# Two attention-and-MLP layers on one core: another table of planner settings, found by a wider search

## The chip, the cores and the metric

The kernel runs on one core of a Trainium2 chip. The metric is device time in microseconds (us) for one execution, and the median of several executions is compared. The measured runs of the kernel before took 1413.7, 1416.55 and 1415.16 us, median 1415.16 us.

## The reference

Input is one sequence of 2048 tokens of 512 features in bf16. Two layers with the same weights follow each other; each is an attention block and an MLP block, both on a layernormed input and both added to the residual:

```
x = x + A(layernorm(x))      # A: 32 heads of 16 features, softmax over 2048 keys, then wo
x = x + B(layernorm(x))      # B: gelu(h @ w1 + b1) @ w2 + b2, 1792 hidden features
x = x + A(layernorm(x))
x = x + B(layernorm(x))
```

Every head needs 2048 x 2048 scores and as many exponentials, twice over. With heads of only 16 features the exponentials weigh as much as the matmuls.

## The kernel before

**The work.** The kernel plans itself when it is built: coroutines put forward operations, a planner (`_Sched.run`, line 517) keeps a clock for each engine, picks the next operation for the engine that can start first, and writes it at the end of that engine's list. On the chip each engine runs its own list in that order, held only by semaphores. So the whole kernel is a static order of some 45,000 instructions, and the planner's choices are its only freedom.

**Cells.** The scores are cut into 4096 cells, in passes. A pass is a layer, a segment of queries (512 of them, the last segment in two halves of 256) and a group of heads; a cell is a pass, one tile of 128 keys and one of four strips of 32 rows of the TensorE array. A cell is one matmul of 512 columns (line 1723, `ps<-qp,kt`) into one bank of PSUM. Its exponential is made in one of two ways:
- On ScalarE (line 2401, `exps`): one ACTIVATE takes the two or three cells of a slot of banks, `128x1024` or `128x1536`, and writes tiles `pt` (or room lent by `kt`, `v` and `g`). There are two such slots, one of three banks and one of two that gets a third bank later.
- On VectorE (line 1997, `dfirst`): a TENSOR_SCALAR turns the scores into 16-bit integers whose bits read as a coarse exponential. Three more planes are made by adding constants to them, mostly on GpSimd (line 2245), a few on VectorE (line 2247). The four planes, each against its own multiple of V (tiles `vc`, line 1651), are summed to the exponential times V.

Then TensorE multiplies by V (line 2468, `pvs`): one matmul for an ACT cell, four for a cell made on VectorE, four side by side in column strips of the array. Projections, wo and the MLP (all line 728, `quads`) run beside attention in the same column strips, some pieces of them in row strips beside the scores (line 1246, `strip`). Where TensorE would be idle, the planner puts in matmuls that compute nothing and keep it busy (line 1711, `fill`); a column strip that has nothing to do in a PV round gets a matmul with zeros (line 2476).

**Words used below.** A slot of TensorE is one stream of 512 columns, by up to four matmuls side by side. A turn is a change between row strips (scores) and column strips (all else). A step is a score group and what stands after it on TensorE up to the next group.

**What sets the order.** 34 constants of the planner (`NAMES`: how many evacuations may be ahead, when a VectorE cell may join a score group, how early PV is taken, and so on) are not constant: `ROWS` holds sets of values, and `PIECES` names the set for each of the 100 equal parts of the 4096 cells. `take` (line 1760) counts scored cells and calls `turn` (line 1756) at each part's end:

```
    def turn(self):
        self.piece += 1
        globals().update(zip(NAMES, ROWS[PIECES[self.piece]]))
```

The kernel before has 45 sets and a list of 100 numbers.

Of the kernel before, what the change touches and what calls it, by code (L numbers as in the profile page):

```python
# [99 lines left out]
         "ALONE", "AHEAD", "PSHIFT", "QUEUE", "SOLO", "BACK", "SIDE", "BOTH", "DMAX", "GMAX", "PMORE", "DUMORE", "GRACE", "PPS", "WAIT", "SOFT",  # L100
         "CLOSE", "LEAST",)
ROWS = (
# [45 lines left out]
)  # L148
PIECES = (36, 37, 18, 29, 2, 43, 11, 29, 41, 15, 37, 38, 0, 37, 31, 25, 13, 23, 16, 40, 30, 37, 25, 29, 6, 13, 0, 16, 13, 14, 44, 0, 4, 15,
          0, 17, 4, 18, 5, 10, 1, 1, 42, 28, 17, 38, 37, 35, 41, 32, 42, 0, 33, 13, 41, 6, 33, 13, 12, 42, 41, 25, 3, 0, 27, 41, 43, 43,  # L150
          19, 8, 37, 6, 38, 16, 33, 6, 36, 37, 20, 35, 41, 21, 24, 37, 7, 4, 9, 15, 25, 24, 8, 21, 37, 22, 31, 34, 26, 12, 39, 31)
CLOSE = 0.35
BOTH = 1
DMAX = 2
# [563 lines left out]
class _Plan:  # L718
# [1041 lines left out]
    def take(self, c):  # L1760
        self.scored += 1
        self.left[c[0]] -= 1
        self.due[c[0]] += 1
        if self.piece + 1 < len(PIECES) and self.scored * len(PIECES) >= (self.piece + 1) * self.total:
            self.turn()
# [823 lines left out]
```

## Time and profile before

| what | us |
|---|---|
| median of the measured runs | 1415.16 (1413.7 to 1416.55) |
| the profiled execution itself | 1413.11 |
| its span, first to last instruction | 1411.3 |
| TensorE (PE) busy | 1382.2, 98% |
| ScalarE (ACT) busy | 1385.1, 98% |
| VectorE (DVE) busy | 1271.7, 90% |
| GpSimd (POOL) busy | 989.7, 70% |

The profiled execution took 2.05 us less than the median, and its span lies 1.8 us inside its own time. PE and ACT are both at 98%, but such a share hides short waits: an ACTIVATE counts as busy until its last result is written, while the next one may start before that. So the distance from one start to the next tells more than the share.

### The profile page before, as it was taken

What the parts mean: (1) busy time and instruction counts of PE and PEld (TensorE: products, weight loads), DVE (VectorE), ACT (ScalarE), POOL (GpSimd) and SP (SyncE); (2) the same over time, 40 slices, a digit from 0 to 9 for tenths busy, and PEclk for the clock granted to TensorE, in tenths of its full rate; (3) what the DMA queues carried; (4) which work ended last, traced back from release to release, by engine and by line L of the source; (5) the groups of instructions that cost most, each with busy time, mean ns of one, the idle gap of its engine ahead of it and who ended that gap; (6) DMA issues with size and microseconds to landing.
All of it is one profiled execution on the core that took longest, in us unless ns stands there. A gap on an engine that the chain in (4) does not pass through costs nothing.

```text
span 1411.3 us, 44915 instructions
## 1 busy us (share of the span) xinstructions
PE 1382.2 (98%) x19487; PEld 411.7 (29%) x19487; DVE 1271.7 (90%) x2500; ACT 1385.1 (98%) x1404; POOL 989.7 (70%) x1239
## 2 busy tenths in 40 slices
PE   8999999999999999999999999999999999999999
PEld 3222222222222222222222222222222222344345
DVE  8999999989999899998999889999988979999794
ACT  7999999999999999999999999999999999999995
POOL 0579787768887588775778868556757874877671
PEclk9999999999999999999999999999999999999999
DMA  5200001124121331114211133101133114101112
GB/s 154 62 2 2 2 2 32 39 77 128 32 62 32 106 98 40 46 39 136 69 35 50 32 114 90 47 16 31 39 103 95 31 44 131 59 20 40 29 36 77
DMA packets 122305, 80.36 MB, mean 57 GB/s; under 512 B 36732, under 2 KB 121084, under 8 KB 122108
## 3 DMA queue, kind: packets, MB, share of 16 engines
q1 hardware_dynamic: 122108, 77.49, 19.5%
q8 instruction: 153, 2.51, 0.7%
q14 instruction: 44, 0.36, 0.1%
HBM read 65.67 MB, written 4.19 MB: 50 GB/s over the span
## 4 chain that ended last, share of the span: by engine, by line
PE 48%; ACT 40%; DVE 11%; POOL 1%; DMA 1%; issue 0%
ACT pt L2401 36%; PE ps L2468 17%; PE ps L1723 16%; PE ps L728 15%; DVE dp L1997 2%; ACT v L2401 1%; DVE kt L1997 1%; DVE v L1997 1%; ACT g L1390 1%; DVE stats L865 1%; ACT g L2401 1%; DVE xln L896 1%; DMA wr<-in_B_w_dram 1%; DVE xf L1997 0%; DVE xt L1089 0%; ACT kt L2401 0%
## 5 line engine op out<-in xcount | busy, mean ns | idle before, releaser
L2401 ACT ACTIVATE pt<-ps 128x1024 bf16<-128x1024 f32 (+1 forms) x1264 | 1236.4, 1153 | 3.7 <-PE ps L1723 2.6
L2245 POOL INT64_ADD dp<-dp x600 | 486.5, 820 | 127.0 <-DVE dp L1997 35.5
L1723 PE MATMUL ps<-qp,kt 32*128 32x512 bf16 x4096 | 547.2, 384 | 10.4 <-ACT pt L2401 7.6
L1997 DVE TENSOR_SCALAR dp<-ps 128x512 uint16<-128x512 f32 x611 | 404.8, 679 | 32.4 <-PE ps L1723 29.5
L1723 PEld LDWEIGHTS ps<-qp,kt 32*128 32x128 bf16 x4096 | 138.0, 91 | 567.7 <-ACT pt L2401 484.4
L2468 PE MATMUL ps<-pt,v 128*17 128x512 bf16 (+1 forms) x3009 | 281.2, 358 | 1.2 <-ACT pt L2401 0.5
L2245 POOL INT64_ADD kt<-kt x235 | 189.9, 812 | 96.2 <-DVE kt L1997 39.0
L2468 PE MATMUL ps<-dp,vc 128*17 128x512 bf16 (+1 forms) x2025 | 222.5, 361 | 1.5 <-POOL v L2245 1.1
L2245 POOL INT64_ADD v<-v x186 | 150.9, 814 | 67.8 <-DVE v L1997 31.2
L1997 DVE TENSOR_SCALAR kt<-ps 128x512 uint16<-128x512 f32 x239 | 160.8, 682 | 20.2 <-PE ps L1723 18.3
L1997 DVE TENSOR_SCALAR v<-ps 128x512 uint16<-128x512 f32 x186 | 124.9, 681 | 14.3 <-PE ps L1723 13.4
L728 PE MATMUL ps<-xf,wr 128*32 128x512 bf16 (+1 forms) x1792 | 128.0, 364 | 0.0
L2468 PE MATMUL ps<-kt,vc 128*17 128x512 bf16 (+1 forms) x897 | 121.2, 338 | 1.2 <-POOL dp L2245 0.9
L728 PE MATMUL ps<-wr,g 128*32 128x512 bf16 x1408 | 105.3, 383 | 0.4 <-DMA wr<-in_B_w_dram 0.2
L2468 PE MATMUL ps<-dp,v 128*17 128x512 bf16 (+1 forms) x675 | 94.6, 361 | 3.8 <-DVE xt L1089 3.1
L2468 PE MATMUL ps<-v,vc 128*17 128x512 bf16 (+1 forms) x654 | 97.1, 350 | 1.0 <-POOL v L2245 0.6
L2245 POOL INT64_ADD q<-q x89 | 72.9, 819 | 32.0 <-DVE q L1997 17.5
L2468 PEld LDWEIGHTS ps<-pt,v 128*17 128x17 bf16 x3009 | 71.1, 88 | 78.0 <-issue 58.3
L2245 POOL INT64_ADD xf<-xf x65 | 53.0, 815 | 51.4 <-DVE xf L1997 36.2
L1372 DVE TENSOR_SCALAR g<-ps,hb1t 128x512 bf16<-128x512 f32 (+1 forms) x112 | 79.0, 707 | 4.9 <-PE ps L728 2.4
L2468 PEld LDWEIGHTS ps<-dp,vc 128*17 128x17 bf16 x2025 | 58.8, 89 | 52.9 <-issue 26.8
L1997 DVE TENSOR_SCALAR q<-ps 128x512 uint16<-128x512 f32 x94 | 63.5, 682 | 8.3 <-PE ps L1723 7.8
(149 smaller groups left out, 1697.7 us busy)
## 6 DMA issues: line engine op xcount, KB each, us to landing
wr<-in_B_w_dram SPq DMA_DIRECT2D x174, 256.0 KB, 3.0
wr<-in_A_wqkv_dram SPq DMA_DIRECT2D x24, 256.0 KB, 3.1
x<-in_A_x_dram SPq DMA_DIRECT2D x7, 512.0 KB, 4.2
wr<-in_A_wo_dram SPq DMA_DIRECT2D x10, 256.0 KB, 3.6
kept<-x SPq DMA_DIRECT2D x4, 512.0 KB, 3.8
x<-kept SPq DMA_DIRECT2D x4, 512.0 KB, 4.1
out_dram<-x SPq DMA_DIRECT2D x16, 128.0 KB, 1.8
q<-in_B_w_dram SPq DMA_DIRECT2D x3, 512.0 KB, 4.4
```

Source lines behind the costliest of these rows:

```text
L728: return [lambda e, a=a: e.matmul(out[32 * a:32 * a + 32, :], lhsT=lhsT[:, 32 * a:32 * a + 32], rhs=rhs, start=start, stop=stop, tile_posi ...
L865: yield _Op("dve", 0.66, lambda e, t=t, src=src: e.bn_stats(T["STATS"][:, t, :], src), reads=[key], writes=["ST.%d" % t], prio=prio)
L896: return _Op("dve", 0.41, lambda e: e.tensor_scalar(T["XLN"][:, x, :], T["X"][:, t % XT, :], T["RSTD"][:, t:t + 1], T["NMR"][:, t:t + 1], ...
L1372: yield _Op("dve", 0.21 + n / 966, lambda e, fc=fc, pb=pb: e.tensor_scalar(T["G"][:, fc, q], pb, T["HB1T"][:, fc:fc + 1], None, op0=ALU.ad ...
L1390: lambda e, g=g: e.activation(out=g, in_=g, func=ACT.Gelu_apprx_tanh), reads=gk, writes=gk, prio=2)
L1723: return (lambda e: e.matmul(o, lhsT=lhsT, rhs=rhs, start=True, stop=True, tile_position=(32 * a, 0)), ["K%d.%d.%d" % (l, gb, kt // 4), "Q ...
L1997: yield _Op("dve", 0.682, lambda e: e.tensor_scalar(u, self.bank(b), E_SCALE, E_BIAS, op0=ALU.mult, op1=ALU.add), reads=["B.%d" % b], writ ...
L2245: op = _Op("pool", PFIX + PWORD * 128 * n * (1 + both), lambda e: e.int64_add(dst, src, by * PACKED), reads=reads, writes=writes)
L2401: yield _Op("act", EXPC + 0.4267 * n, lambda e, src=src, dst=dst: e.activation(out=dst, in_=src, func=ACT.Exp, scale=0.25), reads=["B.%d" ...
L2468: op.fns.append(lambda e, o=o, lhsT=q[0][0][m], rhs=q[0][1][:, n * m:n * m + n], a=a, st=st, sp=sp: e.matmul(o, lhsT=lhsT, rhs=rhs, start= ...
```

## The change

The values in `ROWS` and the list `PIECES` are replaced by those of another search over the planner's settings, one that kept 13 lists and tried 34 candidates at each turn instead of 6 and 28. There are now 47 sets; many are the old ones in other places. No code, no operation and no cost of the planner is touched. Two lines more in the table move every later line down by 2: line 2401 of before is line 2403 of after.

```
 ROWS = (
+    (0.5, 0.1, 0.7, 0.2, 18, 10, 2, 6, 1, 1, 2, 2, 5, 0.3, 0.4, 2, 3.5, 24, 3, 4, 0.4, 1.0, 0, 1, 2, 3, 1, 2, 0.3, 2, 0.15, 0.0, 0.35, 3,),
...
-    (0.5, 0.15, 0.7, 0.2, 18, 10, 2, 6, 1, 1, 2, 2, 5, 0.3, 0.4, 2, 3.5, 24, 3, 4, 0.4, 1.0, 0, 1, 2, 3, 1, 2, 0.3, 2, 0.15, 0.0, 0.35, 99,),
...
-PIECES = (36, 37, 18, 29, 2, 43, 11, 29, 41, 15, 37, 38, 0, 37, 31, 25, 13, 23, 16, 40, 30, 37, 25, 29, 6, 13, 0, 16, 13, 14, 44, 0, 4, 15,
+PIECES = (42, 42, 44, 29, 6, 8, 46, 45, 25, 39, 12, 17, 36, 19, 15, 32, 26, 26, 9, 26, 35, 26, 20, 43, 24, 25, 16, 14, 3, 30, 34, 12, 0,
```

What it does to the engines' lists is shown at three places. The first is ACT's list in the opening, four exponentials behind the last of the three copies of `kt` (line 1005). Before:

```order
L2401 ACTIVATE pt<-ps 128x1536
L2401 ACTIVATE pt<-ps 128x1024 x3
L2401 ACTIVATE pt<-ps 128x1536
L2401 ACTIVATE pt<-ps 128x1024 x4
L2401 ACTIVATE pt<-ps 128x2x512
L2401 ACTIVATE pt<-ps 128x1024 x5
L2401 ACTIVATE pt<-ps 128x2x512
L2401 ACTIVATE pt<-ps 128x3x512
L2401 ACTIVATE pt<-ps 128x2x512
```

The same place after, from the instruction at which the two lists part:

```order
L2403 ACTIVATE pt<-ps 128x3x512
L2403 ACTIVATE pt<-ps 128x2x512
L2403 ACTIVATE pt<-ps 128x1024 x4
L2403 ACTIVATE pt<-ps 128x3x512
L2403 ACTIVATE pt<-ps 128x2x512
L2403 ACTIVATE pt<-ps 128x3x512
L2403 ACTIVATE pt<-ps 128x1024 x6
L2403 ACTIVATE pt<-ps 128x2x512
L2403 ACTIVATE pt<-ps 128x3x512
```

An exponential of three cells (`128x1536` or `128x3x512`) stands here 3 times among 18 before, and 4 times among 17 after. Over the whole list there are 1342 exponentials before (1180 of two cells, 162 of three) and 1337 after (1156 of two, 180 of three, 1 of one).

The second place is ACT's end. `g<-g` is the gelu of the part before the last, which waits until all exponentials are made. Before:

```order
L2401 ACTIVATE pt<-ps 128x1024 x9
L2401 ACTIVATE v<-ps 128x1536 x2
L2401 ACTIVATE pt<-ps 128x1536 x2
L2401 ACTIVATE pt<-ps 128x3x512
L1390 ACT_TABLE_LOAD
L1390 ACTIVATE g<-g 128x7x256 x2
```

After:

```order
L2403 ACTIVATE v<-ps 128x1536 x2
L2403 ACTIVATE pt<-ps 128x1536 x2
L2403 ACTIVATE pt<-ps 128x512
L1392 ACT_TABLE_LOAD
L1392 ACTIVATE g<-g 128x7x256 x2
```

The last exponential takes one cell instead of three; what follows it is the same.

The third place is PE's list from the last score group (`ps<-qp,kt`) on. `17x256` is PV for a segment of 256 queries, so eight of them are one slot. Before:

```order
L1723 MATMUL ps<-qp,kt 128x512 x3
L2468 MATMUL ps<-v,vc 17x256 x2
L2468 MATMUL ps<-pt,v 17x256 x2
L2468 MATMUL ps<-v,vc 17x256 x2
L2468 MATMUL ps<-pt,v 17x256 x2
L2468 MATMUL ps<-v,vc 17x256 x2
L2468 MATMUL ps<-pt,v 17x256 x2
L2468 MATMUL ps<-v,vc 17x256 x2
L2468 MATMUL ps<-pt,v 17x256 x2
L728 MATMUL ps<-xf,wr 32x256 x16
```

After:

```order
L1725 MATMUL ps<-qp,kt 128x512
L2470 MATMUL ps<-pt,v 17x256 x11
L2470 MATMUL ps<-v 17x256
L2470 MATMUL ps<-pt,v 17x256 x3
L2470 MATMUL ps<-v 17x256 x10
L2470 MATMUL ps<-pt,v 17x256 x3
L2470 MATMUL ps<-v 17x256
L2470 MATMUL ps<-pt,v 17x256 x3
L730 MATMUL ps<-xf,wr 32x256 x16
L2470 MATMUL ps<-pt,v 17x256 x8
```

Behind the last score group there were 80 PV matmuls and are now 40; the 592 matmuls of line 728 (730 after) there are the same, and in the same order from the group of 80 `xf,wr` on.

More of the change, by code (lines that the diff above doesn't have):

```diff
@@ L148 @@
 )
-PIECES = (36, 37, 18, 29, 2, 43, 11, 29, 41, 15, 37, 38, 0, 37, 31, 25, 13, 23, 16, 40, 30, 37, 25, 29, 6, 13, 0, 16, 13, 14, 44, 0, 4, 15,
-          0, 17, 4, 18, 5, 10, 1, 1, 42, 28, 17, 38, 37, 35, 41, 32, 42, 0, 33, 13, 41, 6, 33, 13, 12, 42, 41, 25, 3, 0, 27, 41, 43, 43,
-          19, 8, 37, 6, 38, 16, 33, 6, 36, 37, 20, 35, 41, 21, 24, 37, 7, 4, 9, 15, 25, 24, 8, 21, 37, 22, 31, 34, 26, 12, 39, 31)
+PIECES = (42, 42, 44, 29, 6, 8, 46, 45, 25, 39, 12, 17, 36, 19, 15, 32, 26, 26, 9, 26, 35, 26, 20, 43, 24, 25, 16, 14, 3, 30, 34, 12, 0,
+          20, 16, 3, 10, 37, 1, 12, 20, 28, 27, 34, 7, 13, 20, 46, 8, 33, 12, 38, 26, 26, 44, 40, 46, 8, 11, 44, 13, 23, 13, 15, 39, 33,
+          18, 27, 17, 2, 45, 27, 31, 5, 46, 45, 41, 3, 42, 14, 41, 26, 27, 22, 6, 8, 4, 5, 19, 2, 45, 27, 2, 1, 30, 42, 46, 21, 13, 46)
 CLOSE = 0.35
```

32 rows, old and new, of the table ROWS are left out of this document.

## The prediction

> **What bounds the kernel now.** First I read the engines' shares and the chain of work that ended last, on the page:
>
> ```profile
> PE 1382.2 (98%) x19487; PEld 411.7 (29%) x19487; DVE 1271.7 (90%) x2500; ACT 1385.1 (98%) x1404; POOL 989.7 (70%) x1239
> ...
> PE 48%; ACT 40%; DVE 11%; POOL 1%; DMA 1%; issue 0%
> ```
>
> The chain changes between PE and ACT, so neither is simply the bound. The table by stretches (PE, PEld, DVE, ACT, POOL busy, then the granted clock) shows that from the first exponential (12.24) to the end of the last (1383.06) ACT has 3 us of visible idle time in 1370.8, and that PE is full in the tail behind it:
>
> ```profile
> 12.24:700.00 687.76, 677.39 (x8937) 183.70 (x8936) 638.33 (x1250) 685.88 (x695) 501.94 (x627) 1.00 0.20 55
> 700.00:1383.06 683.06, 670.09 (x9858) 207.57 (x9854) 611.75 (x1163) 681.91 (x679) 484.85 (x603) 1.00 0.19 55
> 1383.06:1408.46 25.40, 25.04 (x616) 16.10 (x604) 11.19 (x40) 12.44 (x20) 0.00 (x0) 1.00 0.31 91
> ```
>
> Who waits for whom agrees: score matmuls (line 1723) wait for ACT to free their banks far more than for anything else, 484.4 us in 1158 waits of the weight load.
>
> ```profile
> PEld ps L1723 <- ACT pt L2401: 484.4, 1158, 1.2
> ...
> PEld ps L2468 <- POOL dp L2245: 14.1, 51, 1.4
> ```
>
> So ACT's work, and the short waits between its instructions, set the length of the phase of exponentials. I price both from ACT's instructions in order of time (start, length):
>
> ```profile
> 12.24 3.71 ACT L2401 ACTIVATE pt<-ps 128x1536 bf16<-128x1536 f32 x3 [1.15 <-PE ps L1723]
> 15.82 0.61 ACT L1005 CAST kt<-ps 128x512 bf16<-128x512 f32 x1
> 16.29 4.67 ACT L2401 ACTIVATE pt<-ps 128x1024 bf16<-128x1024 f32 x4
> ...
> 1020.47 1.28 ACT L1390 ACT_TABLE_LOAD   x1
> 1021.76 6.27 ACT L1390 ACTIVATE g<-g 128x3584 bf16<-128x3584 bf16 x2
> 1028.05 1.28 ACT L2401 ACT_TABLE_LOAD   x1
> 1029.35 2.88 ACT L2401 ACTIVATE pt<-ps 128x1024 bf16<-128x1024 f32 x3
> ...
> 1186.33 2.00 ACT L2401 ACTIVATE v<-ps 128x1024 bf16<-128x1024 f32 x2
> 1188.14 4.29 ACT L2401 ACTIVATE pt<-ps 128x1536 bf16<-128x1536 f32 x4
> ...
> 1356.36 1.50 ACT L2401 ACTIVATE v<-ps 128x1536 bf16<-128x1536 f32 x1
> 1357.70 18.49 ACT L2401 ACTIVATE pt<-ps 128x1024 bf16<-128x1024 f32 x20
> 1376.07 2.95 ACT L2401 ACTIVATE v<-ps 128x1536 bf16<-128x1536 f32 x2
> ...
> 1383.06 1.28 ACT L1390 ACT_TABLE_LOAD   x1
> ```
>
> From start to start, two exponentials of two cells take 1.81 us (1186.33 to 1188.14), 0.905 each; one of three takes 1.34; a cell more is thus 0.435. A visit to the gelu takes 8.88 us (1020.47 to 1029.35), a copy 0.47. The 1180 exponentials of two cells (1067.9), 162 of three (217.1), seven gelu visits (62.2) and three copies (1.4) make 1348.6 us. The phase lasted from 12.24 to 1383.06, 1370.8 us. The 22.2 us between are waits, 3 us of them visible and the rest too short to be seen as idle: 0.019 per exponential of two cells. The counts stand in the groups by shape:
>
> ```profile
> L2401 ACT ACTIVATE pt<-ps 128x1024 bf16<-128x1024 f32 x1112 | 1047.0, 1101 | 1.6 <-PE ps L1723 0.6 <-PE ps L2468 0.5
> L2401 ACT ACTIVATE pt<-ps 128x1536 bf16<-128x1536 f32 x152 | 221.0, 1531 | 2.1 <-PE ps L1723 2.0
> ```
>
> (the rest, 38, 22 and 8 of two cells and 2, 5 and 3 of three, writes `kt`, `v` and `g`). Where the waits come from, the chain shows near the end:
>
> ```profile
> 1372.21 0.76 PE ps L2468 x24
> 1372.97 0.33 PE ps L1723 x3
> 1373.30 0.55 PE ps L2468 x16
> ...
> 1380.83 0.32 PE ps L1723 x3
> ...
> 1408.46 0.02 issue
> ```
>
> A step with two slots of PV takes 0.33 + 0.55 = 0.88 us, just under an exponential of two cells. One with three slots takes 1.09, 0.18 over. A slot is 0.21 (0.76 - 0.55), and a score group's 0.32 leaves 0.11 for its turn. Behind the last exponential PE is busy 25.04 of the 25.40 us that are left to its end at 1408.46 (last row of the stretches): the tail is as long as the matmuls left.
>
> **ACT's work: +2.9 us.** The new list has 24 exponentials fewer of two cells (-21.7), 18 more of three (+24.1) and one of a single cell (0.905 - 0.435 = 0.47). VectorE takes 1243 cells instead of 1250, so ACT has 7 more, and the wider exponentials save only the fixed part of five. Gelus, table loads and copies keep their number. As a bound from below, nothing of this can be hidden while ACT is the engine waited for.
>
> The Trainium skill (ScalarE: Activation LUTs, What ACT_TABLE_LOAD costs) gives an ACTIVATE with immediate scale and bias 186 ns + 0.833 ns an element, of which about 93 ns overlap with the next. By that an exponential would come to 0.946 and 1.373 us, and this term to about +2.5, an estimate from that page; the trace has starts 0.905 and 1.34 apart, so more overlaps here, and the trace is used.
>
> **Short waits: -0.4 us.** Counted through PE's list, the steps with three or more slots behind an exponential of two cells are 311 before and 311 after, so the overruns are as many. Steps behind an exponential of three cells have room (1.34 against 0.33 + 0.76 = 1.09). As 24 steps fewer stand behind one of two cells, I take off 24 x 0.019. From below, the run of twenty from 1357.70 to 1376.07 took 18.37 - 18.10 = 0.27 more than its pitch, 0.0135 each; 1337 of that make 18.0, which is 4.2 less than 22.2. From above I take the late planes below, +6.0.
>
> **PE's work: nothing.** Without the idle-time matmuls PE's slots fall from 4747 to 4736 and its turns from 2721 to 2711: 11 x 0.21 + 10 x 0.11 = 3.4 us less. Idle-time slots rise from 144 to 164, 4.2 us that stand in gaps. ACT hides both, and where PE is the bound the 3.4 us would be a gain.
>
> **VectorE, GpSimd, DMA: nothing.** Seven first planes fewer at 0.68 us are 4.8 us off DVE; POOL's shifts fall by 9.
>
> ```profile
> L1997 DVE TENSOR_SCALAR dp<-ps 128x512 uint16<-128x512 f32 x611 | 404.8, 679 | 32.4 <-PE ps L1723 29.5
> ...
> wr<-in_B_w_dram SPq DMA_DIRECT2D x174, 256.0 KB, 3.0
> ```
>
> Both engines have free time (90% and 70%). The 319 issues of SP stay, loaded ahead of their use beside the matmuls; that cover gone, a load that comes late costs at most its landing, 3.0 us.
>
> **The tail: -0.2 us.** Before, the last score group starts at 1380.83, 2.23 us ahead of ACT's last exponential's end (1383.06), and PE needs 27.63 us from there to 1408.46. After, ACT's last exponential has one cell, so the last group stands 0.87 us nearer to ACT's end, and 5 slots fewer (40 PV matmuls) follow: -1.05. Counted from ACT's end the tail goes from 25.40 to 25.40 + 0.87 - 1.05 = 25.22. The bounds are -1.05 (the group comes no later) and +0.9 (nothing else shrinks).
>
> **The sum.** 2.9 - 0.4 - 0.2 = +2.3 us on the profiled 1413.1, so 1415.4. The median of the runs shown, 1415.16, lies 2.05 us above that execution; the forecast for the median is 1417.5, or +0.16%.
>
> **Rival: overruns find room, faster.** An overrun of 0.18 us is absorbed where a light step stands beside it. The new list has more of those: one-slot steps behind two cells go from 39 to 56, and steps of up to three slots behind three cells from 100 to 118. If each of these 35 takes in one overrun, that is 35 x 0.18 = 6.3 us, and the sum is 2.3 - 6.3 = -4.0: 1411.2. For it speak PE's 3.4 us; against it that a run of two-cell exponentials with hardly an overrun, the twenty above, still loses 0.0135 each, so overruns are not the only source. It decides from 29 overruns on (-0.2%).
>
> **Rival: late planes, slower.** PV of a VectorE cell waits for POOL's shifted planes. The waits of the weight load for `dp` are 14.1 us in 51 times, 0.28 each. In a step of two slots there is 0.905 - 0.88 = 0.03 of room, so a wait that falls there reaches ACT with 0.25 us. The place is where PE's and ACT's needs come near each other: in the last fortieth of the cells PE has 125 slots and 67 turns now, 33.6 us, against 34.2 of ACT, where it had 115 slots, 31.5 us against 33.8. If 24 more waits fall in such steps, +6.0: the sum is +8.3, a median of 1423.5; half of them make 1420.5. It decides from 3 waits on, where the time passes +0.2%. Against it: DVE and POOL have less to do than before.
>
> **Rival: the clock, slower.** The stretches above show full clock (1.00), but the kernel's first idle-time matmuls, from 1.1 us on, were slower, 634 ns in the middle against 379 at the least for the same 512 columns:
>
> ```profile
> L1711 PE MATMUL ps<-otn x15: 379/634/634, 1.1 to 6.2; 128*128 128x512 bf16 x15
> ```
>
> PE gets 6 us more room now; one stretch of twenty slots at 255 ns more would cost 5.1 us: 1422.6. The planner's 20 more slots of idle-time matmuls speak against it. The Trainium skill (TensorE: Matmul & The Clock Gate, What's actually happening) has the clock halved after an idle window of about 3.4 us; by that rule a gap alone would do it; the longest of the waits quoted above took 1.4 us.
>
> **How the numbers follow.** I give the forecast 0.50, spread by its bounds; the overruns 0.25, the late planes 0.22, the clock 0.03. Measurement can tell about 0.2%, 2.8 us, from no change. The forecast lies near that border: 0.36 of its 0.50 within, 0.14 above. The overruns give 0.20 faster and 0.05 within; the late planes 0.18 slower and 0.04 within; the clock 0.03 slower. Together: faster 0.20, within 0.45, slower 0.35. The range goes from 1411.0, a little below the overruns' price, to 1422.5, which holds the clock's price nearly and three quarters of the late planes'.
>
> **What would show it.** Right: ACT's exponentials 1156, 180 and 1 by shape, their pitch unchanged, the waits again near 22 us, ACT's last exponential ending some 2.5 us later, and 25.2 us from there to PE's end. The overruns show as waits of 16 us or less at the same pitch. Late planes show as more weight-load waits of line 2470 on POOL and visible idle time before ACTIVATEs; the clock as less than 1.00 in a stretch. The forecast is wrong if the waits change by more than about 3 us either way, since nothing in a list of instructions says how they fall.

## The result, and the profile after

The changed kernel takes **1417.41 us** in the median of 13 runs (1416.42 to 1418.93), the kernel before 1413.91 us in 13 runs beside them (1412.77 to 1416.55). The ratio is 1.0026, with a 95% interval from 1.0018 to 1.0034: slower by 3.5 us. A second comparison, `after_again` below, gave 1.0035 (1.0021 to 1.0048). Weighted by their runs the two make 1.0028, about 4.0 us, and the experiments on the changed kernel are held against that. The forecast was 1417.5 by way of +2.3 us. The median of before was 1413.91 here and 1415.16 in the runs that the forecast started from, so the agreement of the times flatters it; the gap it foresaw was too small by 1.2 to 1.7 us.

The profiled execution of the changed kernel took 1417.95 us (span 1416.2), 4.84 more than that of before. Of that, 1.3 us belong to the two executions: before's lies 0.8 under its median, this one 0.5 above.

The page's engine shares and the shares of the chain that ended last:

```profile
PE 1382.5 (98%) x19519; PEld 413.1 (29%) x19519; DVE 1265.7 (89%) x2492; ACT 1389.0 (98%) x1399; POOL 984.4 (70%) x1230
...
PE 49%; ACT 37%; DVE 10%; DMA 2%; POOL 1%; issue 0%; POOLq 0%; DVEq 0%
```

ACT's busy time grew by 3.9 us, and the chain now has 2% of DMA where it had 1%. The table by stretches (PE, PEld, DVE, ACT, POOL busy, then the granted clock), cut where before's was cut:

```profile
12.24:700.00 687.76, 676.63 (x8921) 184.67 (x8920) 633.41 (x1240) 686.86 (x688) 493.61 (x613) 1.00 0.20 55
700.00:1387.89 687.89, 672.19 (x9907) 208.44 (x9907) 610.40 (x1164) 684.84 (x681) 487.90 (x608) 1.00 0.20 56
1387.89:1413.30 25.41, 24.80 (x608) 15.88 (x600) 11.45 (x41) 12.44 (x20) 0.00 (x0) 1.00 0.17 51
```

The first exponential starts at 12.24 as before, the last ends at 1387.89 instead of 1383.06 (+4.83), and the tail to PE's end is 25.41 where it was 25.40. The whole difference arises in the phase of exponentials, at full clock. ACT's exponentials by shape (count, then busy and mean ns):

```profile
L2403 ACT ACTIVATE pt<-ps 128x1024 bf16<-128x1024 f32 x1094 | 1034.0, 1096 | 2.0 <-PE ps L1725 1.0
L2403 ACT ACTIVATE pt<-ps 128x1536 bf16<-128x1536 f32 x169 | 247.4, 1524 | 2.5 <-PE ps L1725 2.2
...
L2403 ACT ACTIVATE pt<-ps 128x512 bf16<-128x512 f32 x1 | 0.6, 616 | 0.0
```

With those that write `kt` (30 and 3), `v` (24 and 6) and `g` (8 and 2) these are 1156 of two cells, 180 of three and 1 of one, as the prediction counted. By its pitches the phase's work is 1046.2 + 241.2 + 0.5 for them, 62.2 for the gelus and 1.4 for the copies, 1351.5 us: 2.9 more than before. The phase lasted 1375.65, so the waits are **24.2 us**, against 22.2 before: they grew by 2.0, where a fall of 0.4 was forecast. About 1.1 of the 2.0 belongs to this one execution and not to the new order: its undelayed exponentials follow each other 0.8 ns later than before's (0.9042 us for two cells and 1.3309 for three, against 0.9034 and 1.3301), and in another execution of the new order, `after_w2_all` below, they stand at 0.9034 and 1.3301 again, while the old order has 0.9043 in `before_w2_tiny`.

Where they grew is seen when each exponential's start-to-start time is taken less 0.904 us (two cells) or 1.330 (three), the usual pitches of both traces, and summed by hundreds of us. The sums differ by some 1.7 us from the ones above, since the pitches are a little finer.

| waits of ACT, us | 0-100 | 300-400 | 600-700 | 800-900 | 1200-1300 | other nine hundreds | all |
|---|---|---|---|---|---|---|---|
| before | 1.8 | 3.0 | 2.7 | 2.1 | 1.3 | 13.0 | 23.9 |
| changed | 1.0 | 2.0 | 1.7 | **4.5** | 2.6 | 14.1 | 25.9 |

Three places got better by 0.8 to 1.0 us each; 800 to 900 us got worse by 2.4, 1200 to 1300 by 1.3. The gains and the loss at 1200 are there in the second execution of the changed kernel too (`after_again`: 1.0, 2.0, 2.0 and 3.0). The worst place can be looked into. The chain of the changed kernel, between 820 and 847 us:

```profile
821.18 0.32 PE ps L1725 x3
821.50 0.59 PE ps L730 x9
822.09 4.27 DMA wr<-in_B_w_dram
826.36 0.04 issue
826.41 0.61 PE ps L730 x8
...
831.90 0.59 PE ps L730 x9
832.49 4.48 DMA wr<-in_B_w_dram
...
840.99 0.37 PE ps L730 x5
841.36 5.13 DMA wr<-in_B_w_dram
846.50 0.04 issue
846.54 0.64 PE ps L730 x8
```

These are loads of w2 for the first layer's last segment of queries. A load is issued when the matmuls of line 730 have freed one of the four weight buffers, and the matmuls that use it can only start when it has landed, here 4.27 to 5.13 us later. PE had other work for most of that time; what it lacked shows as waits of the weight loads, 0.65, 0.85 and 1.51 us:

```profile
826.40 0.12 PEld L730 LDWEIGHTS ps<-wr,g 128*32 128x32 bf16 x8 [0.65 <-DMA wr<-in_B_w_dram]
837.01 0.12 PEld L730 LDWEIGHTS ps<-wr,g 128*32 128x32 bf16 x8 [0.85 <-DMA wr<-in_B_w_dram]
846.54 0.12 PEld L730 LDWEIGHTS ps<-wr,g 128*32 128x32 bf16 x8 [1.51 <-DMA wr<-in_B_w_dram]
```

Before's chain has no such piece between 800 and 900 us. ACT's instructions in the same stretch (start, length, idle time before):

```profile
829.34 8.38 ACT L2403 ACTIVATE pt<-ps 128x1024 bf16<-128x1024 f32 x9
838.21 9.15 ACT L2403 ACTIVATE pt<-ps 128x1024 bf16<-128x1024 f32 x8 [0.49 <-PE ps L1725]
847.96 1.45 ACT L2403 ACTIVATE pt<-ps 128x1536 bf16<-128x1536 f32 x1 [0.60 <-PE ps L1725]
849.69 1.45 ACT L2403 ACTIVATE pt<-ps 128x1536 bf16<-128x1536 f32 x1 [0.28 <-PE ps L1725]
```

ACT waits for scores that stand in PE's queue behind the late product: 0.49 us at 838.21 and 0.60 and 0.28 behind the third load. The view of the tile `wr` between 800 and 880 us gives the time from issue to landing, first of before, then of the changed kernel:

```profile
DMA to landing us min/median/max: 2.6/3.0/3.8
```

```profile
DMA to landing us min/median/max: 2.6/3.5/5.1
```

It is the landing that changed, hardly the work that stands between an issue and the first use. That work lasts 3.9 us at the least in both kernels (each load of w2 issued between 803 and 846 us, against the first weight load behind it that waits for its semaphore). Before, all 16 of these loads had landed after 3.5 us; now 9 of the 16 took longer. The trace has a landing for each of the 16 parts of a load. Of the load issued at 822.09, 15 parts had landed after 2.60 us and the last one after 4.27; of the one at 832.49, after 2.75 and 4.48. In both cases a packet of 16 KB on the queue that the profile calls `instruction` was under way in between (1.10 us from 824.22 on, 0.95 from 834.43 on). Before has such packets at 822.61, 832.06 and 842.28, each begun ahead of the next load's issue, and there no load's last part lands more than 0.42 us behind its 15th. The queues from the load at 822.09 to its landing, then, in the kernel before, from the load at 823.62 on (packets, MB, share):

```profile
q1 hardware_dynamic: 954, 0.93, 66.5%
q8 instruction: 1, 0.02, 1.6%
```

```profile
q1 hardware_dynamic: 731, 0.71, 60.5%
```

Of the load issued at 841.36 all 16 parts were late (4.99 to 5.13 us); the first of two transposes by DMA was issued 0.55 us behind it, where before has them behind the last load of w2. The changed kernel first, then before:

```profile
841.91 3.96 SPq L913 DMA_TRANSPOSE xp<-xln  x2
```

```profile
847.38 2.50 SPq L911 DMA_TRANSPOSE xp<-xln  x2
```

Over the whole trace of the changed kernel, the last part of a load into `wr` landed over 0.8 us behind the 15th in 18 of the 72 loads that had such an `instruction` packet beside them, and in 2 of the other 136. No run moved these packets or the transposes, so this cause of the late landing is read from the traces and not shown by an experiment.

And the view of the waits in the changed kernel (us, times, longest) has matmuls and weight loads wait for loads of w1 and w2, and more waits for POOL's planes than the 14.1 us in 51 of before:

```profile
PEld ps L1725 <- ACT pt L2403: 478.9, 1155, 1.6
...
PEld ps L2470 <- POOL dp L2247: 19.7, 77, 0.6
...
PEld ps L730 <- DMA wr<-in_B_w_dram: 5.3, 10, 1.5
...
PE ps L730 <- DMA wr<-in_B_w_dram: 2.6, 5, 1.2
```

In the kernel before there is one such line for these loads:

```profile
PEld ps L728 <- DMA wr<-in_B_w_dram: 2.1, 7, 0.5
```

Sums over the whole run are rough, though: in the profiled execution of the control `before_w2_tiny`, below, they are 5.7 us in 15 and 1.7 in 3.

So there are two theories of the loss. **A:** ACT's extra work (+2.9 us) and the late loads (+2) add up. **B:** PE, 98% busy, bounds the phase as much as ACT does, so ACT's work is not what counts, and waits move about.

### The profile page after: what moved, and what is told of

It reads as the page before. It is cut to its first block, busy times and chain, and to the rows that moved or that the text cites. A ratio compares the mean times of both kernels' runs of the same rounds, so it can differ in the third digit from the quotient of the medians.

```text
span 1416.2 us, 44959 instructions
## 1 busy us (share of the span) xinstructions
PE 1382.5 (98%) x19519; PEld 413.1 (29%) x19519; DVE 1265.7 (89%) x2492; ACT 1389.0 (98%) x1399; POOL 984.4 (70%) x1230
## 4 chain that ended last, share of the span: by engine, by line
PE 49%; ACT 37%; DVE 10%; DMA 2%; POOL 1%; issue 0%; POOLq 0%; DVEq 0%
ACT pt L2403 35%; PE ps L2470 18%; PE ps L1725 16%; PE ps L730 15%; DVE dp L1999 2%; DMA wr<-in_B_w_dram 2%; ACT v L2403 1%; DVE kt L1999 1%; DVE v L1999 1%; PE ps L1713 1%; DVE stats L867 1%; ACT g L1392 1%; DVE xt L1091 1%; DVE q L1999 0%; DVE x L1146 0%
## 5 line engine op out<-in xcount | busy, mean ns | idle before, releaser
L2247 POOL INT64_ADD dp<-dp x611 | 495.0, 819 | 141.0 <-DVE dp L1999 37.3
L1999 DVE TENSOR_SCALAR dp<-ps 128x512 uint16<-128x512 f32 x619 | 413.8, 682 | 42.0 <-PE ps L1725 39.2
L2470 PE MATMUL ps<-pt,v 128*17 128x512 bf16 (+1 forms) x3018 | 289.1, 358 | 2.2 <-DVE v L1087 0.5
L2247 POOL INT64_ADD kt<-kt x225 | 182.5, 815 | 89.6 <-DVE kt L1999 30.6
L2470 PE MATMUL ps<-dp,vc 128*17 128x512 bf16 (+1 forms) x2049 | 239.4, 361 | 0.4 <-POOL dp L2247 0.2
L1999 DVE TENSOR_SCALAR kt<-ps 128x512 uint16<-128x512 f32 x226 | 152.0, 683 | 21.5 <-PE ps L1725 19.6
L2470 PE MATMUL ps<-kt,vc 128*17 128x512 bf16 (+1 forms) x852 | 110.7, 337 | 1.9 <-DVE v L2249 1.2
L2470 PEld LDWEIGHTS ps<-dp,vc 128*17 128x17 bf16 x2049 | 62.6, 89 | 50.9 <-issue 26.6
```

The lines of the kernel that those rows point to most:

```text
L1999: yield _Op("dve", 0.682, lambda e: e.tensor_scalar(u, self.bank(b), E_SCALE, E_BIAS, op0=ALU.mult, op1=ALU.add), reads=["B.%d" % b], writ ...
L2247: op = _Op("pool", PFIX + PWORD * 128 * n * (1 + both), lambda e: e.int64_add(dst, src, by * PACKED), reads=reads, writes=writes)
L2470: op.fns.append(lambda e, o=o, lhsT=q[0][0][m], rhs=q[0][1][:, n * m:n * m + n], a=a, st=st, sp=sp: e.matmul(o, lhsT=lhsT, rhs=rhs, start= ...
```

## Experiments

In each, "of before" is the ratio to the kernel before on the same chip, with its 95% interval. Against the changed kernel (1.0028, known to about 0.0007) a difference is known to about 0.0011, or 1.6 us.

**The changed kernel again.** No edit.

> The changed kernel once more, unaltered, beside the runs that are to be compared with it. The first comparison had it 1.0026 of the kernel before (1.0018 to 1.0034); the ratio should come out within that interval.

1.0035 of before (1.0021 to 1.0048), so within the noise of the first. Its profiled execution tells more: ACT's waits sum to 25.6 us, nearly as much as in the first, but lie elsewhere, 2.6 between 800 and 900, 2.1 between 1000 and 1100 (before 1.5), 3.0 between 1200 and 1300. Its chain has late loads of w2 at 822.27 and 840.79, and others at 1055.23, 1064.39, 1084.04 and 1182.55. Where the late loads hurt is thus not the same in every execution.

**The late loads taken away**, in the changed kernel and, as a control, in the one before:

```diff
+        if piece[0] == 0 and piece[1][0] == 3 and piece[2] == "2": dst, src = dst[:, 0:1, 0:64], src[:, 0:1, 0:64]
         yield _Op("sp", SPC, lambda e: e.dma_start(dst, src), ...
```

> The changed kernel, but the fourteen-odd weight loads of w2 for the first layer's last query segment (the ones issued between 804 and 845 us) bring only 128 x 64 elements each, so that the product of that segment is made with stale weights; every instruction stays in its place. Late loads (the theory): in the changed kernel these loads landed after 2.6 to 5.1 us against 2.6 to 3.8 before, PE waited 2.6 us for them in the group of line 730, and nearly all of the 2 us by which ACT's waits grew lies between 800 and 900 us. Smaller transfers land sooner, so about 2 us of the changed kernel's time go, 1.5 to 2.6. ACT's work alone (the rival: the loss is the 2.9 us of exponentials, and waits in one stretch are caught up later): no change, within 0.7 us.

> The same cut of the same weight loads in the kernel before, as a control. Late loads: PE waited only 0.2 us for these loads there, so the time stays within 0.7 us. If smaller transfers help in another way (less traffic beside the other loads), the time falls here by as much as in the changed kernel, and the late loads are not what sets the two kernels apart.

The changed kernel with the small loads is 1.0009 of before (1.0000 to 1.0018): **2.7 us better** than with the whole loads (1.1 to 4.3). The control is 1.0002 (0.9993 to 1.0011), no change. So the late loads of this one segment are worth some 2.7 us, in the changed kernel alone, and theory A's 2.0 lies within that. The visible idle time shows it in the stretch from 800 to 900 us (columns as above); the changed kernel first, then the one with the small loads:

```profile
800.00:900.00 100.00, 96.61 (x1293) 26.96 (x1289) 87.65 (x170) 97.97 (x93) 64.36 (x82) 1.00 0.31 85
```

```profile
800.00:900.00 100.00, 98.75 (x1327) 27.50 (x1315) 89.48 (x173) 99.68 (x97) 66.52 (x85) 1.00 0.16 44
```

PE's busy time in these 100 us goes from 96.61 to 98.75 and ACT's from 97.97 to 99.68. The waits for POOL's planes stayed (19.5 us in 76), so they are not what was won. The whole phase, though, lasted 1375.16 us in this profiled execution, only 0.5 less than with the whole loads: other loads came late at 1053.95 and 1064.64, and ACT waited two times 0.7 us near them. So the 2.7 us rest on the medians.

**All loads of w2 cut**, by the same edit without the first two conditions.

> The changed kernel with every load of w2 into the ring brought down to 128 x 64 elements (stale weights in all products with w2), where the first such run cut only those of one segment. The chain of the changed kernel names late loads of w2 also near 484, 668, 1057, 1064, 1084 and 1183 us. If these cost as the ones at 822 to 841 us do, another 1 to 3 us go beyond the 2 us of the first cut: 3 to 5 us less than the changed kernel. If they fall where nothing waits for PE, it stays at about 2 us less.

1.0009 of before (1.0001 to 1.0018), the same as with one segment's loads cut. Of the two outcomes named it is the second: the other late loads cost nothing that can be measured beyond these. ACT's waits in its profiled execution sum to 23.0 us, 2.9 below the changed kernel's 25.9; 1.1 of that is the 0.8 ns per exponential told above, so 1.8 is left, within the interval of the 2.7 us. Between 1200 and 1300 us it still waits 2.7 us, mostly 0.06 to 0.42 us before the same exponentials as in the changed kernel: the loss of 1.3 there is not of these loads. Which steps make it was not looked into. No control with all loads cut was run on the kernel before.

**ACT's work added, alone.** In the kernel before, exponentials of two cells are cut into four pieces (47 of them with `24 == 5`, 20 with `60 == 5`):

```diff
+            parts = [(j, h) for j in range(n) for h in (0, 256)] if n == 2 and u % 24 == 5 else [None]
-            yield _Op("act", EXPC + 0.4267 * n, lambda e, src=src, dst=dst: e.activation(
-                out=dst, in_=src, func=ACT.Exp, scale=0.25),
+            yield _Op("act", EXPC + 0.4267 * n, [lambda e, x=x, src=src, dst=dst: e.activation(out=dst if x is None else dst[:, x[0]:x[0] + 1, x[1]:x[1] + 256],
+                ..., func=ACT.Exp, scale=0.25) for x in parts],
```

> The kernel before, with 47 of its exponentials of two cells each cut into four of 256 columns: the same output, 141 starts of an instruction more on ACT and nothing else. The pitches 0.905 and 1.34 leave 0.035 us for a start, so ACT's work grows by about 4.9 us; what it grew by is read from the trace. ACT sets the phase (the theory): the time grows by 80 to 100% of ACT's added work, about 4 to 5 us. PE sets it (the rival): it grows by less than 2 us, since ACT's waits take the rest in.

> The kernel before, with only some 20 of its exponentials of two cells cut into four of 256 columns, spread over the run. A piece was 0.264 us from the next in the run with 47 such cuts, so a cut adds 4 x 0.264 - 0.904 = 0.152 us and 20 of them 3.0 us: the size of the term of ACT's work in the prediction (+2.9). ACT's added work counts in full at this size too (the theory): +2.5 to +3.2 us. Small additions find room in ACT's waits of 22 us (the rival, by which the change's +2.9 would be worth less than it was priced at): +0 to +1.5 us.

What a cut costs is read in the run with 47, where one stands by itself, since its four pieces write `g`:

```profile
896.49 1.37 ACT L2402 ACTIVATE g<-ps 128x256 bf16<-128x256 f32 x4
897.54 100.86 ACT L2402 ACTIVATE pt<-ps 128x1536 bf16<-128x1536 f32 x112
```

Four pieces take 1.05 us to the next start instead of 0.904: 0.15 a cut, so 47 of them add 7.0 us and 20 add 3.0. (The 4.9 us expected for the 47 came from a start at 0.035 us; by the undelayed pitches it is 0.05, see the last section.) The time grew by **6.5 us** (1.0046; 1.0033 to 1.0059) and by **2.3 us** (1.0016; 1.0007 to 1.0025; a little less than the 2.5 expected at the least). Within their intervals, ACT's added work counts in full. Theory B's less than 2 us is out for the large dose; the small one, with its interval from 1.0 to 3.5 us, doesn't decide by itself.

**ACT's work taken away, PE's work taken away, and both.** All in the changed kernel:

```diff
-            dst = self.unit(run)
+            m = 508 if u >= 400 and run[-1] < PT_RING else 512; dst, src = self.unit(run)[:, :, 0:m], src[:, :, 0:m]
```

```diff
+        m = out.shape[1] if start or out.shape[1] < 512 else 480
-        return [lambda e, a=a: e.matmul(out[32 * a:32 * a + 32, :], lhsT=lhsT[:, 32 * a:32 * a + 32], rhs=rhs, start=start, stop=stop,
+        return [lambda e, a=a: e.matmul(out[32 * a:32 * a + 32, 0:m], lhsT=lhsT[:, 32 * a:32 * a + 32], rhs=rhs[:, 0:m], start=start, stop=stop, ...
```

> The changed kernel, with 875 of its exponentials (769 of two cells, 105 of three, 1 of one; those from the 400th on whose output lies in the ring pt) 4 columns per cell narrower, so that the last 4 columns of these cells are stale. ACT's work falls by 1854 cells x 4 columns x 0.85 ns (0.435 us for 512) = 6.3 us, spread over the second two thirds. ACT sets the phase (the theory, and the ground of the prediction's term of +2.9): the time falls by 5 to 6.3 us. PE sets it as much as ACT (the rival, since the chain names PE for 48% and PE is 98% busy): the time falls by less than 2.5 us and ACT's waits grow by the rest.

> The changed kernel, with the projections' and MLP's matmuls of line 730 that add to a bank (all but the first of each sum, and those of 512 columns only) cut from 512 columns to 480, so that the last 32 columns of those sums lack these terms. That is 4348 matmuls, 1087 slots, and 1087 x 0.21 x 32/512 = 14.3 us of PE's work, about 1.6 of it behind the last exponential. Both engines bound the phase (the theory since the run with narrower exponentials, where 6 us less of ACT's work were taken up by waits): with PE lighter ACT still has its 1351.5 us of work, so the phase can fall by no more than the 24 us of waits; a PE that is lighter by 12.7 us there takes 2 to 5 us of them away, and the tail 1.6: 3 to 7 us less. ACT alone bounds the phase: 1.6 us less, the tail's. PE alone bounds it: 12 to 14 us less.

> The changed kernel with both cuts at once: 875 exponentials 4 columns per cell narrower (ACT's work -6.0 by the pitches 0.904 and 0.898) and the adding matmuls of line 730 cut to 480 columns (PE's work -14.3). What each leaves out is as in the two runs with one cut. Two engines in balance, each of which takes up what the other saves (the theory): the two together give clearly more than the sum of the two alone (about 0.5 and 4.5 us): 8 to 11 us less than the changed kernel. No such balance (the rival: ACT's cut is worth little for a reason of its own, such as VectorE's or GpSimd's work): the sum, 4 to 6 us.

| cut | work taken away | of before | against the changed kernel |
|---|---|---|---|
| exponentials narrower | ACT 5.7 us | 1.0025 (1.0016 to 1.0033) | -0.5 us |
| matmuls of line 730 shorter | PE 14.3 us | 1.0003 (0.9994 to 1.0011) | -3.6 us |
| both | both | 0.9975 (0.9965 to 0.9985) | -7.6 us |

The exponentials that were cut follow each other by 0.898 and 1.320 us instead of 0.904 and 1.330, so ACT's work fell by 769 x 0.006 + 105 x 0.010 = 5.7 us, somewhat less than the 6.3 estimated. The first run was a miss for theory A, which wanted 5 to 6.3 us: hardly anything of it came back. (Three of its eleven executions had a mean granted clock of 0.998 and took 1420.46 to 1422.55 us; without them the median stays at 1417.6.) The second is within what two balanced engines were expected to give (3 to 7), and far from 14. The two alone make 4.1 us, together they make 7.6, just short of the 8 expected at the least. The difference of 3.5 us is above its noise of about 2.4, though not by much. The phase's rows (columns as above) point the same way for single executions; the changed kernel, then PE's cut, then both. (The profiled execution with ACT's cut alone had half the clock for 6.8 us from 1158.27 on and can't be compared.)

```profile
12.24:1387.89 1375.65, 1348.82 (x18824) 393.12 (x18827) 1243.81 (x2403) 1371.70 (x1368) 981.51 (x1221) 1.00 0.20 55
```

```profile
12.25:1385.05 1372.80, 1343.77 (x18828) 392.75 (x18831) 1243.97 (x2403) 1369.76 (x1368) 983.35 (x1221) 1.00 0.20 55
```

```profile
12.24:1381.53 1369.29, 1340.63 (x18824) 393.62 (x18827) 1242.41 (x2403) 1365.41 (x1369) 981.33 (x1221) 1.00 0.20 55
```

With PE's work alone cut, the phase shortens by 2.85 us, all of it waits, since ACT's work is the same. With ACT's 5.7 cut as well it shortens by 6.36: now 3.5 more, of which some 1.1 is again the 0.8 ns (0.9035 us here, 0.9042 in the other two). So theory B is right where work was taken away: less work on one engine is mostly taken up by the other. Theory A holds where work was added: more work on ACT is not taken up. Work was added only to the kernel before and taken away only from the changed one, so it is not shown that the direction makes the difference, and not the kernel.

**Idle-time matmuls cut short**, in the changed kernel:

```diff
-            fns.append(lambda e, o=o, w=w, a=a, m=m: e.matmul(o, lhsT=w, rhs=rhs, ...
+            r = rhs[:, 0:32] if src == ["B2row"] else rhs[:, 0, 0:32]; o = o[:, 0:32]; fns.append(lambda e, o=o, w=w, a=a, m=m, r=r: e.matmul(o, lhsT=w, rhs=r, ...
```

> The changed kernel, with every idle-time matmul of line 1713 (611 of them, whose products are not used) cut to 32 columns. They stand in PE's gaps (the theory, by which the change's 20 slots more of them cost nothing): the time stays within 0.7 us and the granted clock at 1.00. They delay the matmuls behind them (the rival): up to 164 slots x 0.2 us = 33 us of PE's time come free, and the time falls by some us. They hold the clock up: without them the clock falls below 1.00 in some stretches and the time grows by more than 5 us.

1.0113 of before (1.0096 to 1.0131), 12 us slower than the changed kernel: the third of the three outcomes. Two places in its table of stretches (PE busy, granted clock):

```profile
915.00:920.00 5.00, 3.21 (x60) 1.00 0.00 0
920.00:925.00 5.00, 4.56 (x44) 0.66 0.01 2
1155.00:1160.00 5.00, 2.02 (x89) 1.00 0.01 3
1160.00:1165.00 5.00, 3.69 (x31) 0.55 0.00 0
1165.00:1170.00 5.00, 5.00 (x43) 0.50 0.00 0
```

Each time PE's busy share falls first, and the granted clock in the stretch behind it. So the idle-time matmuls hold the clock up, and whatever they may delay is worth less than that. What the change's 20 slots more of them cost or bring was not measured by itself.

**One part of the change alone.** `PIECES`, with the sets that it names, is taken from the change for the first 64 of the 100 parts (`ab64`) or for the last 36 (`ba64`), and from before for the others. (The diff is shortened to words; the texts below call the parts turns.)

```diff
-PIECES = (36, 37, 18, ...)
+PIECES = the changed kernel's parts 0 to 63, then the parts 64 to 99 of the kernel before   (ab64)
+PIECES = parts 0 to 63 of the kernel before, then the changed kernel's parts 64 to 99       (ba64)
```

> One part of the change alone: the new list's entries for the first 64 turns, the old list's for the other 36. PE's order is the changed kernel's for the first 11424 matmuls, to about 887 us, and its own from there. It has 1147 exponentials of two cells and 188 of three: 1289.9 us by the pitches 0.905 and 1.34, 5.0 more than before. ACT's work and the late loads add up (the theory): +5 for ACT and +2 for the loads, 5.5 to 7.5 us slower than before, and by 887 us it stands 3 to 4 us behind. PE takes ACT's work in where it is the engine waited for: 2 to 4 us slower.

> The other part alone: the old list's entries for the first 64 turns, the new list's for the other 36. PE's order is the kernel before's for the first 11442 matmuls, to about 885 us. It has 1196 exponentials of two cells and 151 of three: 1284.7 us by the pitches, 0.3 less than before, and the weight loads at 805 to 845 us as before. The loss comes from ACT's work and the late loads (the theory): neither is here, so it takes the time of the kernel before, within 2 us. The new rules of the last third lose time by themselves (the rival, late planes towards the end): 2 to 4 us slower than before.

The first part alone: 1.0026 (1.0015 to 1.0037), +3.7 us, less than the 5.5 to 7.5 that A wanted. Its phase (sum of two stretches):

```profile
12.23:700.00 687.77, 676.83 (x8924) 184.83 (x8923) 633.52 (x1241) 686.79 (x688) 493.56 (x614) 1.00 0.20 55
700.00:1387.91 687.91, 670.70 (x9865) 207.98 (x9865) 613.45 (x1169) 685.88 (x679) 474.75 (x594) 1.00 0.20 54
```

It lasted 1375.68 us, 4.86 more than before, and ACT's work is 5.0 more, so the waits are no longer than before's 22.2 on the whole. By hundreds: 800 to 900 us costs 1.4 more than before (3.5 against 2.1), and the gains at 0, 300 and 600 are there as in the changed kernel (2.8 us). A left out these gains. It was right on ACT's work, and the medians' 3.7 has room for 4.86, whose execution of before lies 0.8 low.

The second part alone: 1.0010 (1.0001 to 1.0019), +1.4 us, within the 2 us of A. Yet its profile does not look like that of before: the phase is 4.2 us longer on 0.3 us less of ACT's work, with waits of 3.4 us between 1100 and 1200 (before 1.1), while 26.5 us instead of 28.2 follow to the end of the span. Of these 3.4 us, 1.26 and 0.83 are two single waits, at 1169 and 1113 us; what makes them was not looked into, and that run settles little.

## Why the prediction came out as it did

- **"ACT's work, and the short waits between its instructions, set the length of the phase"**: right for work that was added to the kernel before, which is what the change does. It is wrong as a general sentence: in the changed kernel, 5.7 us less of ACT's work brought 0.5 us alone, and 4.0 on top of PE's cut (7.6 less 3.6).
- **ACT's work, +2.9 us**: right. The counts were 1156, 180 and 1, the pitches unchanged within 0.8 ns, and 3.0 us added by themselves cost 2.3 (1.0 to 3.5). The pitch of 1.34 was read from one pair and held a short wait; by the undelayed 0.9034 and 1.3301 the term is 2.7.
- **Short waits, -0.4 us**: the term that failed, by 2.4 us in the profiled pair; without the 1.1 that are the execution's own, by 1.3. (Its own 24 x 0.019 make 0.46, so -0.5 rather than -0.4.) Counting the steps with three slots or more (311 and 311) caught the overruns, but not what falls on single places: gains of 2.8 us at 0, 300 and 600, losses of 2.4 at 800 and 1.3 at 1200 us.
- **"VectorE, GpSimd, DMA: nothing"**: the step behind a part of it. "The 319 issues of SP stay, loaded ahead of their use beside the matmuls" (the traces have 317 in both) named the cover, and priced its loss at one landing, 3.0 us, but set it at nothing. The cover stayed, 3.9 us at the least in both kernels; what failed is that a landing was taken to stay near 3.0 us. In the new order three loads took 4.27 to 5.13 us to land, weight loads waited 0.65 to 1.51 us for them, and making the loads of that segment small gave 2.7 us back. Of a count of instructions that did not change, the prediction concluded that nothing would be late. The loss of 1.3 us at 1200 to 1300 has another cause, which stays open.
- **PE's work, nothing**: nearly. The cut of 14.3 us was worth 3.6, a quarter, so the 3.4 us less would be worth some 0.9. That is an estimate from that run; it was not measured by itself.
- **The tail, -0.2 us**: it came to 25.41 against 25.40 before. The two effects, which were priced at +0.87 and -1.05, were not measured apart.
- **The sum**, +2.3 us against 3.5 to 4.0: ACT's 2.9, 2.7 of late loads and 1.3 at 1200 to 1300 us make 6.9, and 2.8 came back at the places that got better: 4.1. This split is argued from the table of waits and from a 2.7 that is known to 1.6 us only; it is not shown. That the forecast's 1417.5 lies beside the measured 1417.41 is luck: the start was 1.25 us too high and the gap as much too small.
- **Rivals.** Overruns finding room: not on the whole, the waits grew; whether the gains of 2.8 us at three places are that was not looked into. Late planes: their waits did grow, from 14.1 us in 51 to 19.7 in 77, but with the small loads they stood at 19.5 and the kernel was within 1.3 us (0 to 2.5) of before, so they are not the main cause. The clock: it stayed at 1.00 in all 13 executions of the result. In `after_again` two of five had a mean of 0.998 and took 1419.87 and 1421.56 us, against 1417.62 to 1418.37 for the others, which is part of why that ratio is the higher one. The short idle-time matmuls show that the mechanism is real and that the kernel's own 164 slots of them mostly prevent it.

## What to carry to other kernels

When two engines are both 98% busy, price additions and savings apart: here 7.0 us more on ACT cost 6.5 in one kernel, while 5.7 us less gave 0.5 in the other until PE was lightened too. When a new order keeps the number of loads, set the work between issue and first use, here 3.9 us, against the landing times that occur and not against their median: 3.0 us became up to 5.1 where other transfers ran beside a load, and an order moves those transfers too. And read waits by stretch, not as a sum: a change of 2.0 us was made of five places with both signs, and of 0.8 ns on every exponential that another execution of the same order doesn't have.

## What was not expected of the hardware

- The granted clock fell without a long gap. Within the stretch with 0.66, the trace has it at 0.50 for 3.41 us from 921.55 on. In the 3.41 us before that PE was busy 1.77, and its longest gaps were 0.77 us, ahead of 918.89 and of 920.23. Ahead of 1161.19 it had one gap of 3.80 us, and the clock was 0.50 from 1160.48 on:

```profile
918.14:921.55 3.41, 1.77 (x32) 1.00 0.00 0
921.55:924.96 3.41, 3.32 (x28) 0.50 0.01 2
```

```profile
918.89 0.39 PE L1725 MATMUL ps<-qp,kt 32*128 32x512 bf16 x3 [0.77 <-ACT pt L2403]
920.23 0.40 PE L1725 MATMUL ps<-qp,kt 32*128 32x512 bf16 x4 [0.77 <-ACT pt L2403]
```

```profile
1161.19 0.61 PE L1725 MATMUL ps<-qp,kt 32*128 32x512 bf16 x4 [3.80 <-ACT pt L2403]
```

  The Trainium skill (TensorE: Matmul & The Clock Gate, What's actually happening) has the clock halved after an idle window of about 3.4 us. The second place agrees with that; the first does not, since PE was busy for half of the 3.41 us and no gap there came near it. So a low busy share can be enough.
- A start on ACT costs the same 0.05 us with 256, 1024 and 1536 columns: the undelayed pitches are 0.2642 us (`before_split`), 0.9042 and 1.3309, so 512 columns more take 0.427 and 0.05 is left in each. The 0.435 and 0.035 of the prediction come from the 1.34 that held a wait.
- A load of w2 cut from 256 KB to 16 KB still took 1.6 us at the least from issue to landing, against 2.6 for the whole. And a load can be late by one of its 16 parts alone: 2.60 us for 15 of them, 4.27 for the last.
